# Five edits to a planned attention, expert and gated kernel: first relus on the raw table, a bias half issued later, key low parts by heads, early ups of two kept units, another order of the last tiles

## The chip, the cores and the metric

The kernel runs on one core of a Trainium2 chip. The metric is the time of one execution on the device, in microseconds (us). The kernel before has a median of 791.35 us over three runs (790.55 to 793.41). PE is the matrix engine, PEld its weight loads, DVE the vector engine, ACT the scalar engine, POOL the GpSimd engine, SP the engine whose queue issues nearly all DMAs.

## The reference

Three layers follow each other. Attention has 2 batches, 8 heads, 576 positions and head size 64, with a learned bias on relative distance:

```python
x = (psi_rel / psi_i)[..., None]          # log1p(|i-j|) / log1p(max(i,1))
h = np.maximum(x @ w1 + b1, 0.0)          # 32 hidden units
bias = h @ w2                             # one value per head
scores = scores + bias.transpose(2, 0, 1)[None, :, :, :]
attn = softmax(scores)                    # then attn @ v
```

Its output, 1152 tokens by 512, goes through four experts, `out += p_e * (relu(x @ w1[e]) @ w2[e])` with 1024 hidden units each and normalised weights p, and then through `(x @ w_a * x @ w_b) @ w_out` with 1536 hidden units. All of it is float32.

## The kernel before

**Planner.** `Plan.run` simulates the engines with estimated durations and writes out each engine's instructions in the order it arrives at. Every step is registered by `op` with its engines and their estimates, what it reads and writes, a priority (lower goes first), a number of steps it must come after (`after`) and buffers from rooms that are given out in the order in which they were asked for. On the chip each engine runs its list strictly in order and waits on semaphores only for data. So a change of one step can alter the list of every engine, and an instruction that waits holds all that stand behind it on its engine. DMAs of the SP queue are such a list too.

**Bias.** Since x is a quotient, the hidden layer of one query row is a per-row scale times the relu of w1·log + b1·psi. The log table (`tab`, 128 partitions by 576) is multiplied once by w1. A bias unit `u` is 16 query rows; 36 units make the bias, eight of them (`bias0`) the first 128 rows. `bias_group` makes for each unit four tiles `hh` (4 rows by 32 hidden units on the partitions): on DVE as max(table, −b1·psi), one of the four on ACT as a relu in most units. Four groups of matmuls (`pb`) contract with w2, `put` scales by 1/psi (`rinv`) and adds a correction (`corr`) for the part that max leaves out, `mirror` copies the reversed half, and SP stores the unit to DRAM (`bias_d`). A `bt` tile is read back skewed from there, 128 query rows and two heads; the first one is read in two halves of 64 rows, the first from units 0 to 3, the second from units 4 to 7.

**Attention.** `plain` and `qk_plain` make the first 128 query rows (t = 0) of all 4 pairs of heads and 2 batches from plain float32 keys. The later rows (t = 1 to 4) use keys and queries split into a high and a low part (`keys`, `queries`): a cast `k` and a subtraction for the low part on partitions 64 to 127, with both heads of the pair side by side along 1152 columns. `step` does scores `ps`, DVE adds the bias and takes the minimum of the negated sum (`pr`, `sums`), ACT takes the exponential, PE transposes (`pt`), copies go to `ptb`, and `values` makes `pv`, the product `xf` with the reciprocals, and the high and low parts `x_h`, `x_l` of the layer's output.

**Experts.** A unit of expert weights is 512 KB for the way up and 512 KB for the way down, each split into high and low parts (`wh`, `wl`). `up` multiplies three products of parts, twelve matmuls for 128 hidden units and one stretch of tokens, into one of the `u` banks; `relu` takes the result on ACT (high) and DVE (low, `hl`); `down` makes `pz`, six matmuls per 128 tokens; the sums go to `acc`. Tokens 0 to 255 are the t = 0 rows. Expert work has the priority of filling: PE takes it where nothing of the attention is ready. The two kept units (expert 3, quarters 3 and 2) keep their weights from the first pass to the second; the ups of the second pass for tokens 256 to 511 need only one batch of attention, those for the last 640 tokens need all of it. `x_sums` prepares sums of token blocks on DVE for the units after that (seven products instead of eight).

**Gated layer.** `x2_pair` transposes two 128-token tiles of `acc` (`px`) and makes high and low parts of blocks and of their sums and differences on ACT and DVE; `ab_item` multiplies seven products into `pw`, `pq` and `pr`, lifts them with ACT (`ct<-pw`), combines them on DVE, and `out_item` does the last `pz`. The three pairs of the last 640 tokens (tiles 6, then 4 with 7, then 5 with 8) come first, then two of the first 512 tokens.

Of the kernel before, what the change touches and what calls it, by code (L numbers as in the profile page):

```python
# [9 lines left out]
F32 = mybir.dt.float32  # L10
# [3 lines left out]
ALU = mybir.AluOpType  # L14
# [40 lines left out]
def f(ap):  # L55
    return ap.bitcast(F32)
# [175 lines left out]
def tile_kernel(ctx, tc, qd, kd, kf, vd, cst, probs, w1r, w2r, war, wbr, wor, out):  # L232
# [106 lines left out]
    def scales(e):  # L339
        nc.vector.tensor_scalar(out=pos, in0=neg_.rearrange("p (u g) -> p u g", g=4)[:, :, 4 - pos.shape[2]:], scalar1=cw[:, 1:2], scalar2=None, op0=ALU.mult)  # L340
        nc.vector.tensor_scalar(out=neg_, in0=neg_, scalar1=cw[:, 1:2], scalar2=-1.0, op0=ALU.mult, op1=ALU.mult)
        nc.vector.tensor_scalar(out=w2s, in0=w2s, scalar1=8.0, scalar2=None, op0=ALU.mult)

    lg = Buf(t=cs_t)
    op({"ACT": S / 1.2 + 200}, lambda e: nc.scalar.activation(out=tab, in_=tab, func=AF.Copy, scale=cw[:, 0:1]), r=[cs], w=[lg], prio=-1)
    op({"DVE": 450}, scales, r=[cs], w=[lg])
    cs = lg
# [6 lines left out]

    def corr_copy(e):
        for n, x in corr.items():
            nc.vector.tensor_copy(x, pc.t[:, 0:1])
            for g in range(4 - n, 4):
                nc.vector.memset(x[32 * g:32 * g + 32], 0.0)
# [5 lines left out]
    rows, early = [], []  # L365

    def bias_group(u, rank):
# [3 lines left out]
        for g in range(4):  # L371
            G = 4 * u + g
            hh = new("hh")
            hs.append(hh)
            if g < 4 - acts:
                op({"DVE": n / 1.92 + 130}, lambda e, hh=hh, G=G: nc.vector.tensor_scalar(out=hh.t[:, :n], in0=tab[:, :n], scalar1=neg_[:, G:G + 1], scalar2=None, op0=ALU.max), r=[cs], w=[hh], prio=pri, lock=True)  # L376
            else:
                op({"ACT": n / 1.2 + 220}, lambda e, hh=hh, G=G: nc.scalar.activation(out=hh.t[:, :n], in_=tab[:, :n], func=AF.Relu, bias=pos[:, u, g - 4:][:, :1]), r=[cs], w=[hh], prio=pri)
# [37 lines left out]
        side = op({e: v + 95 for e, v in t_psum(n, ENGINES["side"]).items()}, lambda e: put(e, *ends()[0]), r=[pb, cr], w=[bst], prio=pri)  # L416
# [7 lines left out]
        if u == P // 16 - 1:  # L424
            early.append(o)

# [39 lines left out]
    def bias_tile(m, t):  # L466
# [449 lines left out]
    def w2_item(p, e, c, q, h, prio=RANK["fill"]):  # L916
# [9 lines left out]
        for tt in range(nt):  # L926
# [209 lines left out]
    op({"DVE": 400}, corr_copy, r=[pc], w=[cr])  # L1136
# [50 lines left out]
    for i in (2, 0, 1):  # L1187
        x2_pair(1, i)
# [176 lines left out]
```

## Time and profile before

| | |
|---|---|
| median of 3 runs | 791.35 us (790.55 to 793.41) |
| the profiled execution | 791.38 us, span of its instructions 789.6 us |
| PE busy, matmuls | 774.2 us, 98%, 4933 instructions |
| PEld busy | 662.3 us, 84% |
| DVE / ACT / POOL busy | 649.5 us (82%) / 404.3 us (51%) / 28.1 us (4%) |
| granted PE clock | full speed in every slice |
| chain that ended last | PE 90%, DVE 6%, ACT, DMA and issue 1% each |

Matmuls are pipelined and their ends are modelled, so a busy PE includes some time in which the next matmul was late. The span has four stretches: bias and first attention rows (to about 63 us), the other attention rows among expert work (to 281 us), experts (to about 574 us), the gated layer.

### The profile page before, as it was taken

What the parts mean: (1) busy time and instruction counts of PE and PEld (TensorE: products, weight loads), DVE (VectorE), ACT (ScalarE), POOL (GpSimd) and SP (SyncE); (2) the same over time, 40 slices, a digit from 0 to 9 for tenths busy, and PEclk for the clock granted to TensorE, in tenths of its full rate; (3) what the DMA queues carried; (4) which work ended last, traced back from release to release, by engine and by line L of the source; (5) the groups of instructions that cost most, each with busy time, mean ns of one, the idle gap of its engine ahead of it and who ended that gap; (6) DMA issues with size and microseconds to landing.
All of it is one profiled execution on the core that took longest, in us unless ns stands there. A gap on an engine that the chain in (4) does not pass through costs nothing.

```text
span 789.6 us, 13146 instructions
## 1 busy us (share of the span) xinstructions
PE 774.2 (98%) x4933; PEld 662.3 (84%) x4933; DVE 649.5 (82%) x1374; ACT 404.3 (51%) x848; POOL 28.1 (4%) x46
## 2 busy tenths in 40 slices
PE   7998999999999999999999999999999999999997
PEld 3475678888988888888888888889889999999996
DVE  7899986889896687998989998988698985757545
ACT  6877765677766543544544535344466532433321
POOL 0000100000000000000000000010010100000000
PEclk9999999999999999999999999999999999999999
DMA  6996658677563134455545653545405340301103
GB/s 233 327 344 215 232 178 276 218 243 244 179 208 98 45 96 127 134 166 175 160 126 159 204 175 120 166 132 161 134 1 183 112 160 1 107 27 55 54 1 120
DMA packets 46432, 120.31 MB, mean 152 GB/s; under 512 B 5024, under 2 KB 9376, under 8 KB 46368
## 3 DMA queue, kind: packets, MB, share of 16 engines
q1 hardware_dynamic: 46224, 119.34, 46.6%
q8 instruction: 39, 0.64, 0.3%
q14 instruction: 25, 0.20, 0.1%
q10 hardware_dynamic: 144, 0.13, 0.0%
HBM read 93.62 MB, written 25.84 MB: 151 GB/s over the span
## 4 chain that ended last, share of the span: by engine, by line
PE 90%; DVE 6%; ACT 1%; issue 1%; DMA 1%; DVEq 0%; ACTq 0%
PE pz L785 32%; PE up L883 14%; PE pw L1030 9%; PE up L772 8%; PE pb L390 4%; PE pv L613 4%; PE pr L1030 4%; PE ps L513 4%; PE pt L548 4%; PE pq L1030 2%; PE ps L531 1%; PE pz L1110 1%; DVE pr L516 1%; DVE k L453 1%; PE rp L593 1%
## 5 line engine op out<-in xcount | busy, mean ns | idle before, releaser
L785 PE MATMUL pz<-wh,hh 128*128 128x512 f32 x386 | 153.2, 397 | 0.0
L785 PE MATMUL pz<-wh,hl 128*128 128x512 f32 x386 | 151.3, 392 | 0.0
L785 PE MATMUL pz<-wl,hh 128*128 128x512 f32 x386 | 151.2, 392 | 0.0
L785 PEld LDWEIGHTS pz<-wl,hh 128*128 128x128 f32 x386 | 72.5, 188 | 15.9
L785 PEld LDWEIGHTS pz<-wh,hh 128*128 128x128 f32 x386 | 72.5, 188 | 14.2 <-issue 1.8
L785 PEld LDWEIGHTS pz<-wh,hl 128*128 128x128 f32 x386 | 72.5, 188 | 12.2
L239 ACT COPY ct<-pw 128x640 f32<-128x640 f32 (+3 forms) x48 | 27.9, 582 | 85.0 <-PE pw L1030 85.0
L516 DVE CUSTOM_DVE_ANT_0 pr<-ps,bt 128x576 f32<-128x576 f32 (+1 forms) x80 | 59.9, 753 | 13.9 <-PE ps L513 11.3
L658 DVE TENSOR_TENSOR wl<-wst,wh 128x1024 fp32r<-128x1024 f32 (+1 forms) x60 | 69.7, 1162 | 1.9 <-ACT wh L239 1.6
L526 ACT ACTIVATE pr<-pr,sums 128x576 f32<-128x576 f32 x72 | 56.1, 780 | 15.3 <-DVE sums L516 10.4
L772 PE MATMUL up<-x_h,wh 128*128 128x256 f32 (+1 forms) x200 | 61.7, 308 | 0.7 <-DVE hl L796 0.7
L239 ACT CAST wh<-wst 128x1024 fp32r<-128x1024 f32 (+1 forms) x56 | 54.5, 974 | 15.1 <-PE pz L785 7.8
L772 PE MATMUL up<-x_h,wl 128*128 128x256 f32 (+1 forms) x200 | 57.3, 286 | 0.0
L772 PE MATMUL up<-x_l,wh 128*128 128x256 f32 (+1 forms) x200 | 57.2, 286 | 0.0
L239 ACT COPY ptb<-pt 128x512 f32<-128x512 f32 (+3 forms) x98 | 40.3, 438 | 30.8 <-PE pt L548 25.4
L376 DVE TENSOR_SCALAR hh<-cs 128x560 f32<-128x560 f32 (+17 forms) x112 | 43.9, 448 | 3.8 <-PE pb L390 3.6
L239 ACT COPY ct<-up 128x448 f32<-128x448 f32 x39 | 20.7, 531 | 47.8 <-PE up L883 47.6
L613 PE MATMUL pv<-ptb,v 128*64 128x128 f32 (+2 forms) x480 | 44.1, 331 | 0.3 <-ACT bst L408 0.3
L883 PE MATMUL up<-xb,wsh 128*128 128x448 f32 x156 | 44.3, 365 | 0.0
L1125 DVE TENSOR_TENSOR acc<-pz,acc 128x512 f32<-128x512 f32 x44 | 30.2, 689 | 15.9 <-PE pz L785 14.9
L772 PEld LDWEIGHTS up<-x_h,wh 128*128 128x128 f32 x200 | 37.6, 188 | 6.5 <-issue 3.0
L548 PE MATMUL pt<-ident,pr 128*128 128x128 f32 x288 | 41.7, 275 | 0.0
(194 smaller groups left out, 1844.8 us busy)
## 6 DMA issues: line engine op xcount, KB each, us to landing
wst<-in_w1r SPq DMA_DIRECT2D x30, 512.0 KB, 4.4
wst<-in_w2r SPq DMA_DIRECT2D x30, 512.0 KB, 4.5
bias_d<-bst SPq DMA_DIRECT2D x36, 295.5 KB, 4.1
bt<-bias_d SPq DMA_DIRECT2D x15, 576.0 KB, 5.3
v<-in_vd SPq DMA_DIRECT2D x24, 320.0 KB, 4.3
s<-in_war SPq DMA_DIRECT2D x12, 512.0 KB, 4.9
wz_d<-hl SPq DMA_DIRECT2D x24, 256.0 KB, 2.5
s<-in_wbr SPq DMA_DIRECT2D x12, 512.0 KB, 4.9
```

The source lines that it names most:

```text
L239: (nc.scalar.copy if e == "ACT" else engine[e].tensor_copy)(out, in_)
L376: op({"DVE": n / 1.92 + 130}, lambda e, hh=hh, G=G: nc.vector.tensor_scalar(out=hh.t[:, :n], in0=tab[:, :n], scalar1=neg_[:, G:G + 1], sca ...
L390: nc.tensor.matmul(t[32 * g:32 * g + 32, o + lo:o + hi], w2s, hs[g].t[:, lo:hi], start=True, stop=True)
L516: nc.vector.tensor_tensor_reduce(out=pr.t[r0:r1, c].rearrange("p (a b) -> p a b", a=2), in0=ps.t[r0:r1, :, :HS], in1=bt.t[r0:r1, c].rearra ...
L526: nc.scalar.activation(out=pr.t[:, c], in_=pr.t[:, c], func=AF.Exp, scale=-1.0, bias=sums.t[:, neg:neg + 1], accum_out=sums.t[:, col:col + 1])
L548: nc.tensor.transpose(pt.t[:, kt * P:kt * P + P], pr.t[:, s, k0:k0 + P], ident)
L613: nc.tensor.matmul(pv.t[s * D:(s + 1) * D, :w], V.t[:, s, kt * D:(kt + 1) * D], ptb.t[:, blk, :w], start=(kt == 0), stop=(kt == 4))
L658: op(t_two(1024 - skip, ENGINES["wlo"]), lambda e: engine[e].tensor_tensor(out=w.t[1][:, skip:], in0=wst.t[:, skip:], in1=f(w.t[0][:, skip ...
L772: nc.tensor.matmul(u.t[:, :n], block(a, ft, d), x_at(x, d, lo, n), start=(d == 0 and j == 0), stop=(d == 3 and j == 2))
L785: nc.tensor.matmul(z.t, a[:, ft, tt * P:(tt + 1) * P], bb[:, ft, :], start=(first and ft == 0 and j == 0), stop=(final and ft == 1 and j = ...
L883: nc.tensor.matmul(bank.t[:, :n], s(a, k), x(b, k), start=(first and k == 0 and i == 0), stop=(stop and k == 1 and i == 2), skip_group_che ...
L1030: nc.tensor.matmul(o_, s[:, k], d[:, k], start=(first and k == 0 and i == 0), stop=(k == 1 and i == 2), skip_group_check=True)
```

## The change

Names: `raw` is the log table as it is loaded, `tab` now a tile of its own.

1. The first bias unit takes the raw table: DVE multiplies by w1 and takes the maximum in one instruction, ACT multiplies inside its relu. The scaled table is made on ACT after that relu, for units 1 to 35. −b1·psi goes to a tile of its own, b1·psi (`pos`) moves from DVE to ACT. The factor 8 moves from w2 to `rinv` and `corr`; the zeros of `corr` are set on POOL at the start.
2. The read of the first `bt` half is registered as coming after the store of unit 6.
3. The subtraction for the low part of the keys is two steps, one for each head, 576 columns each.
4. For the first kept unit the ups of tokens 256 to 511 of both kept units are registered before the ups of the last 640 tokens.
5. The downs of the last unit of the second pass take the last five tiles in the order 4, 7, 6, 5, 8 instead of 4 to 8, and the pairs of `x2_pair` follow as (4, 7), 6, (5, 8).

```diff
+    psi, neg_ = neg_, hp.tile([P, NG], F32, name="neg")
+    op({"DVE": 290}, lambda e: nc.vector.tensor_scalar(out=neg_, in0=psi, scalar1=cw[:, 1:2], scalar2=-1.0, op0=ALU.mult, op1=ALU.mult), r=[cs], w=[NEG], prio=-1)
+    op({"ACT": 250}, lambda e: nc.scalar.activation(out=pos, in_=psi.rearrange("p (u g) -> p u g", g=4)[:, :, 4 - pos.shape[2]:], func=AF.Copy, scale=cw[:, 1:2]), r=[cs], w=[POS], prio=-1)
+    op({"DVE": 90}, lambda e: nc.vector.tensor_scalar(out=rinv, in0=rinv, scalar1=8.0, scalar2=None, op0=ALU.mult), r=[cs], w=[RI], prio=0.1)
+    raw, tab = tab, hp.tile([P, S], F32, name="tab")
+    def table():
+        op({"ACT": S / 1.2 + 200}, lambda e: nc.scalar.activation(out=tab, in_=raw, func=AF.Copy, scale=cw[:, 0:1]), r=[cs], w=[lg], prio=-0.5, after=first)
...
     def corr_copy(e):
         for n, x in corr.items():
-            nc.vector.tensor_copy(x, pc.t[:, 0:1])
-            for g in range(4 - n, 4):
-                nc.vector.memset(x[32 * g:32 * g + 32], 0.0)
+            nc.vector.tensor_scalar(out=x[:P - 32 * n], in0=pc.t[:P - 32 * n, 0:1], scalar1=8.0, scalar2=None, op0=ALU.mult)
...
+            if u == 0 and g < 4 - acts:
+                op({"DVE": n / 1.92 + 190}, lambda e, hh=hh, G=G: nc.vector.tensor_scalar(out=hh.t[:, :n], in0=raw[:, :n], scalar1=cw[:, 0:1], scalar2=neg_[:, G:G + 1], op0=ALU.mult, op1=ALU.max), r=[cs, NEG], w=[hh], prio=pri, lock=True)
+            elif u == 0:
+                first.append(op({"ACT": n / 1.2 + 220}, lambda e, hh=hh, G=G: nc.scalar.activation(out=hh.t[:, :n], in_=raw[:, :n], func=AF.Relu, scale=cw[:, 0:1], bias=pos[:, u, g - 4:][:, :1]), r=[cs, POS], w=[hh], prio=pri))
+                table()
...
+        if u == P // 16 - 2:
+            sixth.append(o)
...
-        op(t_two(2 * S, ENGINES["ksub"]), lambda e: engine[e].tensor_tensor(out=k.t[D:P], in0=k2.t[D:P], in1=f(k.t[D:P]), op=ALU.subtract), r=[k2], rw=[k], prio=RANK["prep"], lock=True)
+        whole = list(k.writers)
+        for s in range(2):
+            op(t_two(S, ENGINES["ksub"]), lambda e, s=s: engine[e].tensor_tensor(out=k.t[D:P, s], in0=k2.t[D:P, s], in1=f(k.t[D:P, s]), op=ALU.subtract), r=[k2], w=[k], after=whole, prio=RANK["prep"], lock=True)
...
-                op({"SP": 440}, lambda e, h=h, r=r: nc.sync.dma_start(out=bt.t[r], in_=bias_rows(D * h, D, 0, 2)), r=rows[4 * h:4 * h + 4], w=[bt], size=D * 8 * S)
+                op({"SP": 440}, lambda e, h=h, r=r: nc.sync.dma_start(out=bt.t[r], in_=bias_rows(D * h, D, 0, 2)), r=rows[4 * h:4 * h + 4], w=[bt], size=D * 8 * S, after=sixth)
...
-        for tt in range(nt):
+        for tt in (0, 3, 2, 1, 4) if p and c == 2 and last and e == es[-1] else range(nt):
...
-                weights(1, e, q)
-                h1[q] = w1_item(1, e, 1, q)
+                for x in KEPT if (e, q) == KEPT[0] else [(e, q)][(e, q) in KEPT:]:
+                    weights(1, *x)
+                    h1[x[1]] = w1_item(1, e, 1, x[1])
...
-    for i in (2, 0, 1):
+    for i in (0, 2, 1):
         x2_pair(1, i)
```

DVE at its start, from the first instruction after the tables have landed (`pos` and `cs` are written from the constants' tile; `hh` are the bias tiles of units 0 and 1). Before:

```order
L340 TENSOR_SCALAR pos<-cs 128x36
L341 TENSOR_SCALAR cs<-cs 128x144
L342 TENSOR_SCALAR cs<-cs 128x32
L376 TENSOR_SCALAR hh<-cs 128x576 x3
L376 TENSOR_SCALAR hh<-cs 128x560 x4
L357 COPY corr_101<-pc 128x1
L357 COPY corr_102<-pc 128x1
L359 MEMSET corr_102 32x1
```

The same stretch of DVE in the changed kernel:

```order
L341 TENSOR_SCALAR neg<-cs 128x144
L343 TENSOR_SCALAR cs<-cs 128x36
L380 TENSOR_SCALAR hh<-cs,neg 128x576 x3
L363 TENSOR_SCALAR corr_101<-pc 128x1
L363 TENSOR_SCALAR corr_102<-pc 96x1
L385 TENSOR_SCALAR hh<-tab,neg 128x560 x4
```

Three small instructions became two, the first three `hh` read the raw table, and the correction stands before unit 1 instead of behind it.

The SP queue from the first values to the full bias tiles (`bias_d<-bst` are the stores of the units in order, the 64-row `bt` the two halves). Before:

```order
L633 DMA v<-in_vd 128x640 x2
L421 DMA bias_d<-bst 128x591 x6
L487 DMA bt<-bias_d 64x2x576
L421 DMA bias_d<-bst 128x591 x4
L487 DMA bt<-bias_d 64x2x576
L476 DMA bt<-bias_d 128x2x576 x2
```

The same stretch of SP in the changed kernel:

```order
L646 DMA v<-in_vd 128x640 x2
L430 DMA bias_d<-bst 128x591 x9
L500 DMA bt<-bias_d 64x2x576
L430 DMA bias_d<-bst 128x591
L500 DMA bt<-bias_d 64x2x576
L489 DMA bt<-bias_d 128x2x576 x2
```

The first half moved from behind the store of unit 5 to behind that of unit 8; the second half stays behind the store of unit 9.

DVE at the end of the t = 0 rows (`xf`, `x_h`, `x_l` belong to the last heads of t = 0, `k` to the split keys; ISA `pr` is the first sum of scores and bias with t = 1). Before:

```order
L461 TENSOR_TENSOR ql<-q_747,qh 128x512
L376 TENSOR_SCALAR hh<-cs 128x320
L239 CAST k<-k_756 128x1152
L376 TENSOR_SCALAR hh<-cs 128x320
L453 TENSOR_TENSOR k<-k_756,k 64x1152
L618 TENSOR_TENSOR xf<-pv,rb 128x128
L376 TENSOR_SCALAR hh<-cs 128x320
L239 CAST x_h<-xf 128x128
L376 TENSOR_SCALAR hh<-cs 128x336
L621 TENSOR_TENSOR x_l<-xf,x_h 128x128
L516 ISA pr,sums<-ps,bt 128x576
```

The same stretch of DVE in the changed kernel:

```order
L634 TENSOR_TENSOR x_l<-xf,x_h 128x128
L385 TENSOR_SCALAR hh<-tab,neg 128x304
L239 CAST k<-k_763 128x1152
L385 TENSOR_SCALAR hh<-tab,neg 128x304
L466 TENSOR_TENSOR k<-k_763,k 64x576 x2
L385 TENSOR_SCALAR hh<-tab,neg 128x320 x2
L466 TENSOR_TENSOR k<-k_772,k 64x576
L809 SCALAR_TENSOR_TENSOR hl<-up,hh 128x256
L466 TENSOR_TENSOR k<-k_772,k 64x576
L529 ISA pr,sums<-ps,bt 128x576
```

The last `x_l` of t = 0 stood five instructions behind the keys' low part and now stands ahead of the keys' cast; an `hl` of expert work stands among the low parts of the second keys.

On PE the changed list has 24 up matmuls between the last `pv` of t = 0 and the first `ps` with t = 1, where the list before has none; 36 stand before the second `ps`, where before it had 6. At the end of the attention 42 fill matmuls stand between the last `pv` and the first up of the last 640 tokens, where before there were none. In the gated layer the last `px` of the 640 tokens is followed by 24 `pz` matmuls before the first `pw`, where before it was 42. The put of unit 7 moves from DVE to ACT and its mirror from ACT to DVE.

## Rows read from the trace of the kernel before

**Rows 1.** Page, part 1: busy time and share of PE, PEld.

```profile
PE 774.2 (98%) x4933; PEld 662.3 (84%) x4933; DVE 649.5 (82%) x1374; ACT 404.3 (51%) x848; POOL 28.1 (4%) x46
```

**Rows 2.** Windows: stretch, length, busy PE PEld DVE ACT POOL, clock, DMA share.

```profile
30.00:60.00 30.00, 29.75 (x304) 20.95 (x302) 28.93 (x99) 24.66 (x64) 0.85 (x2) 1.00 0.99 352
60.00:70.00 10.00, 7.69 (x74) 6.19 (x70) 9.74 (x26) 8.53 (x18) 0.41 (x1) 1.00 0.59 218
70.00:130.00 60.00, 60.00 (x467) 42.39 (x468) 49.87 (x107) 41.91 (x79) 6.03 (x11) 1.00 0.65 219
300.00:580.00 280.00, 280.00 (x1350) 244.23 (x1349) 248.40 (x483) 127.07 (x247) 2.34 (x2) 1.00 0.49 150
```

**Rows 3.** Waits of PE, whole span: sum, times, longest.

```profile
PE pc L353 <- DVE cs L342: 4.8, 1, 4.8
...
PE ps L513 <- DVE k L453: 1.1, 1, 1.1
```

**Rows 4.** Timeline of DVE and ACT from 4 us: start, duration.

```profile
4.02 0.25 DVE L340 TENSOR_SCALAR pos<-cs 128x36 f32<-128x36 f32 x1 [4.02 <-DMA cs<-in_cst]
4.31 0.29 DVE L341 TENSOR_SCALAR cs<-cs 128x144 f32<-128x144 f32 x1
...
4.83 3.06 DVE L376 TENSOR_SCALAR hh<-cs 128x576 f32<-128x576 f32 x7
...
4.02 0.78 ACT L345 ACTIVATE cs<-cs 128x576 f32<-128x576 f32 x1 [1.79 <-DMA cs<-in_cst]
```

**Rows 5.** Groups by form: two DVE operations with constants; one with a per-partition scalar.

```profile
L688 DVE TENSOR_SCALAR t<-t 128x512 f32<-128x512 f32 x36 | 16.1, 451 | 0.8 <-ACT t L702 0.7
L376 DVE TENSOR_SCALAR hh<-cs 128x512 f32<-128x512 f32 x6 | 2.6, 480 | 0.2 <-PE pb L390 0.2
```

**Rows 6.** Timeline of SP and DVE: first half, store of unit 7, second half, first scores.

```profile
18.51 0.71 SPq L487 DMA_DIRECT2D bt<-bias_d  x1
...
19.90 0.42 SPq L421 DMA_DIRECT2D bias_d<-bst  x1
...
24.21 0.61 SPq L487 DMA_DIRECT2D bt<-bias_d  x1
...
28.15 0.76 DVE L516 CUSTOM_DVE_ANT_0 pr<-ps,bt 128x576 f32<-128x576 f32 x1 [1.96 <-DMA bt<-bias_d]
```

**Rows 7.** DMA issues, KB, us to landing: store of unit 0, then of unit 7.

```profile
bias_d<-bst SPq DMA_DIRECT2D x1, 295.5 KB, 2.1
...
bias_d<-bst SPq DMA_DIRECT2D x1, 295.5 KB, 4.2
```

**Rows 8.** Timeline of PE and DVE at the end of t = 0.

```profile
62.91 0.53 PE L513 MATMUL ps<-k,qh 128*128 128x288 f32 x2 [1.14 <-DVE k L453]
...
64.97 0.53 PE L513 MATMUL ps<-k,qh 128*128 128x288 f32 x2 [0.58 <-DVE sums L516]
...
61.50 1.35 DVE L453 TENSOR_TENSOR k<-k,k 64x1152 fp32r<-64x1152 f32 x1
...
63.83 0.29 DVE L621 TENSOR_TENSOR x_l<-xf,x_h 128x128 fp32r<-128x128 f32 x1
```

**Rows 9.** Chain in order of time: 24 ups of 256 tokens; 24 downs.

```profile
132.76 2.83 PE up L772 x24
...
613.59 5.48 PE pz L785 x24
```

**Rows 10.** Timeline of PE: an up after the attention's end.

```profile
286.94 0.42 PE L772 MATMUL up<-x_h,wh 128*128 128x320 f32 x1 [0.46 <-DVE hl L796]
```

**Rows 11.** Timeline of PE and DVE: last pair of the 640 tokens, first products, lift.

```profile
563.50 0.82 PE L970 MATMUL px<-ident,acc 128*128 128x128 f32 x6
...
571.88 0.68 DVE L996 TENSOR_TENSOR x_l<-px,x_h 128x512 fp32r<-128x512 f32 x1
...
573.74 0.30 PE L1030 MATMUL pw<-x_h,wh 128*128 128x320 f32 x1
...
585.49 0.42 PE L1030 MATMUL pw<-x_h,wh 128*128 128x320 f32 x1 [1.06 <-ACT ct L239]
```

More of the change, by code (lines that the diff above doesn't have):

```diff
@@ L337, in tile_kernel @@
     op({"SP": 440}, lambda e: nc.sync.dma_start(out=cs_t, in_=cst), w=[cs], size=P * 3160)
[L339 to L347, printed above, removed]
+    psi, neg_ = neg_, hp.tile([P, NG], F32, name="neg")
+    NEG, POS, RI = Buf(t=neg_), Buf(t=pos), Buf(t=cs_t)
+    op({"DVE": 290}, lambda e: nc.vector.tensor_scalar(out=neg_, in0=psi, scalar1=cw[:, 1:2], scalar2=-1.0, op0=ALU.mult, op1=ALU.mult), r=[cs], w=[NEG], prio=-1)
+    op({"ACT": 250}, lambda e: nc.scalar.activation(out=pos, in_=psi.rearrange("p (u g) -> p u g", g=4)[:, :, 4 - pos.shape[2]:], func=AF.Copy, scale=cw[:, 1:2]), r=[cs], w=[POS], prio=-1)
+    op({"DVE": 90}, lambda e: nc.vector.tensor_scalar(out=rinv, in0=rinv, scalar1=8.0, scalar2=None, op0=ALU.mult), r=[cs], w=[RI], prio=0.1)
+    raw, tab = tab, hp.tile([P, S], F32, name="tab")
+    lg = Buf(t=tab)
+    def table():
+        op({"ACT": S / 1.2 + 200}, lambda e: nc.scalar.activation(out=tab, in_=raw, func=AF.Copy, scale=cw[:, 0:1]), r=[cs], w=[lg], prio=-0.5, after=first)
+    first = []
     pc, cr = new("tv", "pc"), Buf(t=cs_t)
@@ L353, in corr_mm @@
             nc.tensor.matmul(pc.t[32 * g:32 * g + 32, 0:1], w2s, cw[:, 1:2], start=True, stop=True)
+    for n, x in corr.items():
+        nc.gpsimd.memset(x, 0.0)
     def corr_copy(e):
         for n, x in corr.items():
-            nc.vector.tensor_copy(x, pc.t[:, 0:1])
-            for g in range(4 - n, 4):
-                nc.vector.memset(x[32 * g:32 * g + 32], 0.0)
+            nc.vector.tensor_scalar(out=x[:P - 32 * n], in0=pc.t[:P - 32 * n, 0:1], scalar1=8.0, scalar2=None, op0=ALU.mult)
     def dist(u):
@@ L363, in dist @@
         return before, after, max(before + 1, after)
-    rows, early = [], []
+    rows, early, sixth = [], [], []
     def bias_group(u, rank):
@@ L374, in bias_group @@
             hs.append(hh)
-            if g < 4 - acts:
-                op({"DVE": n / 1.92 + 130}, lambda e, hh=hh, G=G: nc.vector.tensor_scalar(out=hh.t[:, :n], in0=tab[:, :n], scalar1=neg_[:, G:G + 1], scalar2=None, op0=ALU.max), r=[cs], w=[hh], prio=pri, lock=True)
+            if u == 0 and g < 4 - acts:
[3 more added lines that the diff above has]
+                table()
+            elif g < 4 - acts:
+                op({"DVE": n / 1.92 + 130}, lambda e, hh=hh, G=G: nc.vector.tensor_scalar(out=hh.t[:, :n], in0=tab[:, :n], scalar1=neg_[:, G:G + 1], scalar2=None, op0=ALU.max), r=[lg, NEG], w=[hh], prio=pri, lock=True)
             else:
-                op({"ACT": n / 1.2 + 220}, lambda e, hh=hh, G=G: nc.scalar.activation(out=hh.t[:, :n], in_=tab[:, :n], func=AF.Relu, bias=pos[:, u, g - 4:][:, :1]), r=[cs], w=[hh], prio=pri)
+                op({"ACT": n / 1.2 + 220}, lambda e, hh=hh, G=G: nc.scalar.activation(out=hh.t[:, :n], in_=tab[:, :n], func=AF.Relu, bias=pos[:, u, g - 4:][:, :1]), r=[lg, POS], w=[hh], prio=pri)
         pb = new("tv" if n <= 512 else "s", "pb")
@@ L415, in bias_group @@
         m = min(before, after - 1)
-        side = op({e: v + 95 for e, v in t_psum(n, ENGINES["side"]).items()}, lambda e: put(e, *ends()[0]), r=[pb, cr], w=[bst], prio=pri)
+        side = op({e: v + 95 for e, v in t_psum(n, ENGINES["side"]).items()}, lambda e: put(e, *ends()[0]), r=[pb, cr, RI], w=[bst], prio=pri)
         op({e: v for e, v in {"POOL": 2 * m + 150, "ACT": m / 1.2 + 95, "DVE": m / 0.96 + 68}.items() if e in ENGINES["mirror0" if rank == "bias0" else "mirror"].split()}, mirror, w=[bst], after=[side], prio=pri)
@@ L1135, in tile_kernel @@
     op({"PE": 600}, corr_mm, r=[cs], w=[pc])
-    op({"DVE": 400}, corr_copy, r=[pc], w=[cr])
+    op({"DVE": 200}, corr_copy, r=[pc], w=[cr])
     for u in range(NU):
```

## The prediction

> **What bounds the kernel now.** I read the page's busy times first: PE is busy 98% of the span, so only 789.6 − 774.2 = 15.4 us of idle time is visible [rows 1]. Then the windows, to see where it lies. From 300 to 580 us PE is busy without a break and its weight loads take 244.23 of 280 us, 87% [rows 2]: there is nothing to win there. From 60 to 70 us PE is busy for 7.69 of 10 us while DVE is busy for 9.74, and from 30 to 60 us DVE has 28.93 of 30 us and the DMA engines a share of 0.99 [rows 2]. So the first stretch belongs to DVE and the transfers, the long rest to PE. The waits of PE name the single stalls: 4.8 us until the tables are there, 1.1 us for the keys' low part [rows 3]; the timelines give the others. The clock stands at 1.00 in every stretch shown [rows 2], so no step is priced for it.
>
> A time saved before about 63 us moves everything behind it, if PE has work at once; a time saved later counts only where PE waits. PE's instructions are the same in number and shape in both kernels, so the sum is one of waits.
>
> **First relus on the raw table.** The tables land at 4.02. DVE makes three small scalings and then stands until ACT has scaled the table (0.78 us), so its first maximum starts at 4.83 [rows 4]. Now it makes two small scalings; the first of them cost 4.31 − 4.02 = 0.29 from start to start [rows 4], so the maxima start at about 4.5, 0.3 earlier. Against that each of the three has a second scalar read per partition, a form that the trace lacks on operands in on-chip memory. The nearest row is an operation with two constants, 451 ns for 512 columns, where one with a single per-partition scalar takes 480 [rows 5]: the second step of arithmetic is free there. If the second scalar halved the rate, each would double: seven take 3.06, 0.44 each [rows 4], so three would lose 1.3 us. I take 0.1 in all, by the nearest row. The scaled table is needed after these three, at about 5.9; ACT makes its small scaling, its relu and the table, 0.25 + 0.78 + 0.78 behind 4.02 by the durations of like rows [rows 4], done at 5.8. It is hidden, with 0.1 us to spare; where it isn't, DVE waits by tenths. Net 0.2 us, between −1.0 and 0.5. The zeros of the correction on POOL, the factor 8 on other tiles and the correction ahead of unit 1 replace as much as they add.
>
> **The bias half behind more stores.** The first scores start on DVE at 28.15, after 1.96 us of waiting for the second half of the bias tile [rows 6]. That half is issued at 24.21, because it needs the store of unit 7 to have landed: issued at 19.90, it took 4.2 us, to 24.1 [rows 6, 7]. The first half's read stood right ahead, issued at 18.51 and holding SP for 0.71 [rows 6]. The store of unit 0, ahead of any read of the bias, landed in 2.1 us [rows 7]. In the new list the read goes behind the store of unit 8, so unit 7's has only stores ahead. It can't go much earlier, though: its put is now on ACT behind a relu, and its mirror waits on DVE. I put it at 19.7, and its landing between the two rows, at 3.3 us: 23.0. So the second half goes 1.2 us earlier and the scores 1.1 us earlier, the 0.2 of the table included in the 19.7. At most it is 28.15 − 1.96 = 26.2, when DVE is out of work: 2.0 us. At least nothing, if the first half, now issued at about 21.6, delays the second as it delayed the stores before. What follows from 30 to 60 us runs on transfers (share 0.99, [rows 2]) that all stand behind these halves on SP, so it moves with them. **Term 1: 1.1 us (0 to 2.0).**
>
> The Trainium skill, DMA: Bandwidth & Descriptors, section "Anatomy of one DMA", says that some 2 us of a DMA are fixed, mostly the receipt for the write, and heaviest where HBM is the target. The 2.1 us of unit 0 agrees, the 4.2 of unit 7 doesn't [rows 7]. By the rule as the whole cost the second half would go at about 22, and the term would be 2.0; I keep 1.1, from the rows.
>
> **Key low parts by heads.** PE waits 1.14 us at 62.91 for the low part, one instruction of 1.35 us for both heads, and 0.58 us at 64.97 for DVE [rows 8]. The split alone would let the first head go 0.67 earlier at the price of one more small start on DVE. But the larger change is in the order. Before, the last `x_l` of t = 0 is written at 63.83, behind the low part [rows 8], so no up could be finished earlier; now it stands ahead of the cast, and PE has 24 ups between the last `pv` and the first scores with t = 1. 24 ups take 2.83 us [rows 9]; PE was idle for 10 − 7.69 = 2.31 us in this stretch [rows 2]. The ups aren't free of waits: there are two banks for them, and the third set of twelve waits for an `hl` that stands on DVE behind three low parts of 0.67 each; with it the second scores wait, queued behind these twelve. So I count not 2.83 but most of the idle time, 2.0 us. At most 36 ups, 4.2 us by the same row, are gained; at least nothing, if DVE (83% busy from 70 to 130 us by 49.87 of 60, [rows 2]) sets the pace of what follows and PE stands later for what it gained now. **Term 2: 2.0 us (0 to 4.2).**
>
> **Both kept units' ups first.** Before, the ups of the last 640 tokens follow the last `pv` directly, while DVE makes sums of tokens; one up waits 0.46 us for an `hl` [rows 10]. With 42 matmuls in between, the conversions have time. **Term 3: 0.5 us (0 to 0.9).**
>
> **Order of the last tiles.** Before, the `px` of the last pair start by 563.50; its first low part starts at 571.88, ends at 572.56, and the first product goes at 573.74, behind 42 downs [rows 11]: 8.6 us from the end of the `px` (564.0), of which the pair spends most in line behind the other two. Now there are only 24 downs, 5.48 us [rows 9], for it. If the 8.6 stayed, PE would stall 3.1 us. But the pair of two tiles comes first now and is converted while 18 downs run, so the last one should find ACT and DVE free: I take no stall. Later, at 585.49, PE waits 1.06 us for a lift on ACT behind casts [rows 11]. In the new lists the difference that those casts need comes earlier; a lift itself can't be hidden there, so I take 0.4 of it. **Term 4: 0.4 us (−3.1 to 1.1).**
>
> **Sum.** 1.1 + 2.0 + 0.5 + 0.4 = 4.0. The profiled execution took 791.38 us (span 789.6), the median of the runs is 791.35: the sum goes against 791.4 and gives 787.4 us. What a measurement here can tell from no change is about 0.5%, 4.0 us: the forecast lies on that bound.
>
> **Rivals.** *The gain at 60 us is given back.* DVE and ACT feed the attention until about 130 us, and PE's lead over them shrinks as buffers fill. For it: DVE's 9.74 of 10 us [rows 2]. Against it: 83% afterwards, and expert work that needs little of DVE. Term 2 is then about 0.2, and the time 791.4 − 2.2 = 789.2.
>
> *PE has more slack than its busy time shows.* From 70 to 130 us PE counts as busy for all 60 us, but its weight loads for only 42.39, 71% against 87% later [rows 2]; that would be up to 9 us in which matmuls came late, though the bias's matmuls load only 32 columns of weights and explain part. A new order with an early lead of PE may close some: term 2 reaches 4.2, and the time is 791.4 − 6.2 = 785.2. The Trainium skill, Perfetto Trace Analysis, section "Identifying the Most-Contended Engine", says that busy matmuls are a poor measure of PE's headroom and the share of weight loads a good one. These two rows bear it out.
>
> *The attention falls behind and the fill runs out (the other side).* The ups now stand ahead of scores in PE's list. If each of the 16 later groups lost the wait computed above for the third twelve, about 0.9 us (three low parts of 0.67 less a first block of scores and the products between), the attention would end 14 us late; 42 matmuls, some 6 us, are left as fill. PE would idle 8 us before the last ups: 791.4 − 1.1 − 0.4 + 8 = 797.9. It makes the kernel slower from a lateness of about 8 us on. For it: one up waits there already [rows 10]. Against it: fewer matmuls stand ahead of the last `pv` than before.
>
> *The edits do little.* The first half delays the second where it now stands, and the last pair stalls PE by up to 3.1: 791.4 − 2.0 − 0.5 + 3.1 = 792.0 at worst, about 791 in the middle.
>
> **How the numbers follow.** The forecast has 0.45, half of it either side of its bound (own range 785.8 to 789.0): 0.24 faster, 0.21 same. Given back: 0.18, same. More slack: 0.17, faster. Little: 0.08, same. Attention late: 0.12, of which 0.11 slower and 0.01 same. So faster by over 0.5% 0.41, within 0.5% 0.48, slower 0.11. The range runs from 784.6, a little under the second rival, to 791.6, over the first and most of the last; what lies outside is the late attention and the tails, under 0.2.
>
> **What would show it.** Right: first scores on DVE at about 27.0; the second half issued near 23; PE from 60 to 70 us busy for 9 us or more, without a wait over 0.3 for the keys; no wait at the first ups of the last 640 tokens; first `pw` directly behind the downs. Wrong: a doubled duration of the three maxima on the raw table; the second half issued at 24 or landing after 28; PE waiting for `hl` between 60 and 130 us by more than 2 us in all; a wait of `pw` for `x_l` near 570 us; the last `pv` later than 281 us.

## The result: slower by 4.9 us, where 4.0 us less was predicted

The changed kernel takes 796.86 us (median of 6 runs, 795.60 to 799.43), the kernel before 791.97 us beside it (6 runs, 790.55 to 793.41). The ratio is 1.0061, with a 95% interval from 1.0045 to 1.0076. The forecast was 787.4 us and its range ended at 791.6. A median mixes executions with and without a short fall of PE's clock (last section): of 94 of the kernel before, the 35 with a mean clock of 0.998 or less have a median of 792.8 us, the others 791.2.

The page of the changed kernel (columns as in [rows 1]), from an execution of 798.19 us with a span of 796.4:

```profile
PE 779.2 (98%) x4933; PEld 663.0 (83%) x4933; DVE 651.5 (82%) x1398; ACT 401.3 (50%) x834; POOL 32.2 (4%) x45
```

PE has the same 4933 matmuls and seems as busy as before, 98%. That row hides the loss, since a matmul that comes late counts as busy. The windows show more (columns as in [rows 2]):

```profile
28.00:30.00 2.00, 0.70 (x4) 0.34 (x5) 1.56 (x5) 0.76 (x2) 0.00 (x0) 1.00 1.05 393
30.00:31.00 1.00, 1.00 (x8) 0.61 (x7) 1.00 (x3) 1.00 (x5) 0.00 (x0) 0.93 1.05 391
31.00:32.00 1.00, 1.00 (x7) 1.00 (x6) 0.97 (x6) 1.00 (x3) 0.00 (x0) 0.50 1.09 412
32.00:34.00 2.00, 2.00 (x9) 1.37 (x9) 0.94 (x4) 1.44 (x4) 0.00 (x0) 0.50 1.00 356
...
60.00:70.00 10.00, 9.17 (x86) 7.23 (x83) 9.67 (x27) 7.41 (x16) 0.00 (x0) 1.00 0.74 283
70.00:130.00 60.00, 59.27 (x459) 39.90 (x457) 52.01 (x114) 46.37 (x90) 8.78 (x10) 1.00 0.71 231
130.00:200.00 70.00, 67.75 (x511) 58.48 (x511) 59.49 (x141) 43.85 (x99) 2.67 (x4) 1.00 0.67 214
```

The last stretch in the kernel before:

```profile
130.00:200.00 70.00, 69.85 (x525) 61.80 (x524) 62.44 (x128) 47.87 (x115) 1.94 (x3) 1.00 0.76 246
```

The hole from 60 to 70 us is filled, 9.17 us busy against 7.69. But from 70 to 200 us PE does fewer matmuls (970 against 992), loads weights for 98.4 us against 104.2, and stands still for 3.0 us against 0.15. The first scores didn't come earlier either. SP, then DVE (start, duration; answers to [rows 6]; the first row holds the stores of units 7 and 8, the third the tenth store, that of unit 9):

```profile
19.56 1.56 SPq L430 DMA_DIRECT2D bias_d<-bst  x2
21.22 0.71 SPq L500 DMA_DIRECT2D bt<-bias_d  x1
23.73 0.33 SPq L430 DMA_DIRECT2D bias_d<-bst  x1
24.23 0.61 SPq L500 DMA_DIRECT2D bt<-bias_d  x1
...
28.43 0.76 DVE L529 CUSTOM_DVE_ANT_0 pr<-ps,bt 128x576 f32<-128x576 f32 x1 [1.79 <-DMA bt<-bias_d]
```

The second half goes at 24.23, as before, though the store of unit 7 had landed at 21.65. It stands on SP behind the tenth store, and that one waited for the mirror copy of its unit, which the new list has put on POOL. POOL's copy, and SP's wait for it from 15 to 25 us:

```profile
21.98 1.73 POOL L239 COPY bst<-bst 128x159 f32<-128x159 f32 x1 [20.59 <-ACT bst L417]
SPq L430 <- POOL bst L239: 1.8, 1, 1.8
```

In the kernel before ACT made this copy, and the tenth store went at 22.24:

```profile
21.89 0.33 ACT L239 COPY bst<-bst 128x159 f32<-128x159 f32 x1
```

The waits of PE over the whole span (answer to [rows 3]) are many small ones on what DVE and ACT make:

```profile
PE pc L356 <- DMA cs<-in_cst: 4.3, 1, 4.3
PE up L785 <- DVE hl L809: 2.0, 3, 0.9
PE ps L544 <- issue: 1.5, 1, 1.5
PE pw L1043 <- DVE ct L1068: 1.0, 1, 1.0
PE pw L1043 <- ACT ct L239: 0.8, 1, 0.8
PE pv L626 <- DVE ptb L239: 0.7, 2, 0.4
```

One of them shows how such a wait comes about. DVE and PE from 129 us, in the changed kernel:

```profile
129.49 0.69 DVE L239 CAST wh<-wst 128x1024 fp32r<-128x1024 f32 x1 [2.16 <-PE up L785]
130.10 1.22 DVE L671 TENSOR_TENSOR wl<-wst,wh 128x1024 fp32r<-128x1024 f32 x1
131.23 0.75 DVE L809 SCALAR_TENSOR_TENSOR hl<-up,hh 128x256 fp32r<-128x256 f32 x2
131.71 0.39 PE L785 MATMUL up<-x_h,wh 128*128 128x256 f32 x1 [0.85 <-DVE hl L809]
```

PE has filled both banks with ups. The `hl` that would free one is ready to be computed at 129.9, but the list has put a weight's cast and low part ahead of it on DVE, and PE stands for 0.85 us. DVE was not short of time here: it had itself stood for 2.16 us before that cast, until PE's ups were through. It is the order that costs here.

**A measure that counts late matmuls.** For the comparisons below I cut PE's instructions into blocks of one operation and shape. A block lasts until the next one starts. Its excess is that time less its count times the pace of the fastest fifth of such blocks in the trace before. The excess of a stretch holds waits, slow starts and a lower clock alike. In us, by stretch:

```
              0-28  28-36 36-60 60-70 70-200 200-280 280-300 300-560 560-640 640-  sum
before        15.1   1.3   3.1   3.1   15.9    7.0     1.4     3.4     3.8   2.4  56.6
after         15.9   2.4   2.7   1.3   21.9    7.8     0.4     3.9     4.5   3.0  63.8
start_only    15.9   1.1   2.3   2.1   20.6    6.4     0.4     3.8     4.6   2.7  59.9
split_only    14.2   1.4   3.5   3.2   19.3    6.9     1.3     3.8     2.8   2.8  59.1
kept_only     13.9   1.4   4.1   3.0   16.0    7.0     1.1     3.9     5.0   3.0  58.3
tiles_only    14.9   1.3   3.1   3.1   16.1    6.9     1.4     3.2     4.0   2.8  56.8
n_settle      14.9   2.6   3.4   2.5   21.2    7.5     0.5     3.3     3.0   2.9  61.9
n_corr        14.1   1.4   4.2   1.5   19.7    7.3     0.4     3.2     2.9   2.9  57.5
n_act149      14.7   1.3   3.2   4.0   17.9    7.7     0.7     3.3     3.0   2.6  58.3
raw_held      15.0   1.5   4.2   2.9   16.0    7.0     1.4     3.4     3.8   2.9  58.2
split_held    14.1   1.4   3.5   2.7   15.9    7.1     1.3     3.5     3.6   2.8  55.7
half_first    14.3   1.2   2.1   2.9   20.7    7.7     0.2     3.8     3.6   2.9  59.4
hyb_a         14.0   1.4   4.1   3.0   16.1    6.9     1.4     3.4     3.7   2.7  56.6
lite_before   14.8   1.3   3.7   1.9   15.0    6.7     1.2     3.5     3.5   2.8  54.5
lite_after    16.0   1.1   2.3   2.9   19.3    6.8     0.2     3.3     4.1   2.9  58.7
raw_only      16.2   2.2   2.7   1.6   21.0    6.3     0.6     3.3     4.9   2.8  61.7
hyb_b         14.6   1.4   3.5   2.7   16.2    7.1     1.2     3.4     3.6   2.8  56.5
hyb_c         15.7   1.3   3.1   3.0   16.1    6.9     1.4     3.2     3.7   2.8  57.2
```

The sums differ by 7.2 us between before and after, the two executions by 6.8. Of that 6.0 us lie from 70 to 200 us, in the attention with its fill, where the prediction had no term. From 60 to 70 us 1.8 us are won, from 280 to 300 us 1.0. How far one trace can be trusted, the table shows too: the eight in which PE has the list of before up to 200 us with nothing taken from its work (before, kept_only, tiles_only, raw_held, split_held and the three hyb) lie between 15.9 and 16.2 from 70 to 200 us. Two traces of another list there differ by more: 21.9 and 20.7 (after, half_first), 20.6 and 21.0 (start_only, raw_only).

### The profile page after: what moved, and what is told of

Read it like the earlier page. It is cut to its first block, busy times and chain, and to the rows that moved or that the text cites. A ratio compares the mean times of both kernels' runs of the same rounds, so it can differ in the third digit from the quotient of the medians.

```text
span 796.4 us, 13154 instructions
## 1 busy us (share of the span) xinstructions
PE 779.2 (98%) x4933; PEld 663.0 (83%) x4933; DVE 651.5 (82%) x1398; ACT 401.3 (50%) x834; POOL 32.2 (4%) x45
## 4 chain that ended last, share of the span: by engine, by line
PE 87%; DVE 7%; DMA 2%; ACT 2%; issue 2%; DVEq 0%; SPq 0%
PE pz L798 32%; PE up L896 13%; PE pw L1043 9%; PE up L785 8%; PE pv L626 4%; PE pr L1043 4%; PE pb L399 4%; PE pt L561 4%; PE ps L526 4%; PE pq L1043 2%; PE ps L544 1%; DMA wst<-wz_d 1%; DVE pr L529 1%; PE pz L1123 1%; DVE wl L671 1%
## 5 line engine op out<-in xcount | busy, mean ns | idle before, releaser
L798 PEld LDWEIGHTS pz<-wl,hh 128*128 128x128 f32 x386 | 72.4, 188 | 15.9
L239 ACT CAST wh<-wst 128x1024 fp32r<-128x1024 f32 (+1 forms) x54 | 52.3, 968 | 13.1 <-PE pz L798 8.8
L808 ACT ACTIVATE hh<-up 128x256 fp32r<-128x256 f32 (+2 forms) x76 | 27.8, 381 | 41.2 <-PE up L785 30.2
L385 DVE TENSOR_SCALAR hh<-tab,neg 128x544 f32<-128x544 f32 (+17 forms) x109 | 42.0, 443 | 4.4 <-PE pb L399 4.3
L239 ACT COPY ct<-up 128x448 f32<-128x448 f32 x39 | 20.7, 531 | 49.3 <-PE up L896 49.2
## 6 DMA issues: line engine op xcount, KB each, us to landing
bias_d<-bst SPq DMA_DIRECT2D x36, 295.5 KB, 3.6
```

The lines of the kernel that those rows point to most:

```text
L239: (nc.scalar.copy if e == "ACT" else engine[e].tensor_copy)(out, in_)
L798: nc.tensor.matmul(z.t, a[:, ft, tt * P:(tt + 1) * P], bb[:, ft, :], start=(first and ft == 0 and j == 0), stop=(final and ft == 1 and j = ...
```

## The experiments

All times are medians; a ratio is against the kernel before in the same session (791.39 to 791.96 us).

**Each part alone.** The change's diff was put on the kernel before piece by piece: the raw table with the bias half behind the seventh store (start_only), the raw table without that (raw_only), the key's low part by heads (split_only), both kept units' ups first (kept_only), the order of the last tiles and pairs (tiles_only).

```diff
# raw_only differs from start_only by
-                op({"SP": 440}, ..., r=rows[4 * h:4 * h + 4], w=[bt], size=D * 8 * S, after=sixth)
+                op({"SP": 440}, ..., r=rows[4 * h:4 * h + 4], w=[bt], size=D * 8 * S)
```

> The kernel before with the raw-table relus and the bias half behind seven stores, nothing else. Theory A (the loss of 4.9 us sits in the order of the fill work between 100 and 282 us and is not made by the start): the first scores stay near 28.4 us, so 791 to 793, with a dip of the granted clock near 31 us in some executions worth 2 to 3 us. Rival B (the start makes the loss, by the clock and by what it delays): 794.5 to 797.5.

> The raw-table relus alone; PE and DVE keep the list of the run with both parts of the start, only the bias half goes behind six stores and not nine. Theory A: the same as start_only within 1 us, because the second half's landing decides the first scores and stays at 28 to 28.5 us. Rival (the half behind nine stores costs or gains by itself): a difference of 1 us or more, in the sense of where the second half lands.

> The kernel before with the key low parts by heads, nothing else; the list of PE changes from its 299th instruction. Theory A: the changed order of the fill loses what the split gains, 793 to 796. Rival B: 789 to 791, the 2 us that PE was idle from 60 to 70 us.

> The kernel before with the ups of both kept units first, nothing else; PE's list changes only from its 1687th instruction. Theory A: no wait at the first ups of the last 640 tokens, but a changed order of the fill: 791 to 794. Rival B: 790.5 to 791.5, the 0.5 us alone.

> The kernel before with the order of the last tiles and of the last three pairs alone; PE's list is that of before up to its 3057th instruction. Theory L (lists cost; here little is dealt anew): the stretch 560 to 640 us moves by -0.4 to +1.3 us, the rest not, 791.0 to 792.7. Rival P (the new order of the pairs by itself brings the wait behind the weights' sums near 624 us): 792.4 or more.

Measured: start_only 794.47 (1.0042, 1.0027 to 1.0057); raw_only 795.17 (1.0047, 1.0030 to 1.0063); split_only 793.78 (1.0034, 1.0023 to 1.0046); kept_only 793.35 (1.0019, 1.0009 to 1.0028); tiles_only 790.95 (0.9987, 0.9977 to 0.9997). All but the last are slower, by 1.8 to 3.6 us, and they don't add up: start, split and kept together would be 6.9. Theory A put the loss on the order of the fill and left the start at 791 to 793; the start alone costs 2.9, so that form of it fell. The number is nearly rival B's (from 794.5), but not its reason: the loss is not at the start. To 28 us there is 0.8 more excess, from 70 to 200 us 4.7 more, and the clock stood at 1.0 in all four runs. split_only loses 3.4 in that stretch. kept_only leaves it alone, as its list differs only later, and loses 1.2 from 560 to 640 us. So the same stretch loses from edits that have nothing in common but that the planner then hands out another list. (raw_only lies within 1 us of start_only and split_only and kept_only in their ranges, all as theory A had it; tiles_only is just below theory L's range.) That called for lists without any edit.

**New lists, no edit.** One number of the planner is changed. PE's instructions stay the same, but by a comparison of the lists some 700 to 760 of them stand elsewhere, about as many as with the start alone (some 720) or the split alone (some 650). What the planner hands out includes the engine for some of the small steps: DVE has 1380 instructions in n_settle, 1375 in n_corr and 1393 in n_act149, where before it has 1374, and ACT and POOL have that many fewer in sum. So "not one instruction is altered", below, holds for the steps and not for where each runs.

```diff
-    SETTLE = {"PE": 210, "ACT": 150, "DVE": 140, "POOL": 120}
+    SETTLE = {"PE": 210, "ACT": 150, "DVE": 141, "POOL": 120}   # n_settle
+    SETTLE = {"PE": 210, "ACT": 149, "DVE": 140, "POOL": 120}   # n_act149
-    op({"DVE": 400}, corr_copy, r=[pc], w=[cr])
+    op({"DVE": 200}, corr_copy, r=[pc], w=[cr])                 # n_corr
```

> The kernel before with one number of the planner raised by 1 ns (what it adds behind each instruction of DVE); not one instruction is added, removed or altered, but the planner hands out another list, in which some 700 of PE's instructions stand elsewhere, as many as with the start alone or the split alone. Theory L (the list is what costs: the one of before is a lucky one, and any edit deals a new one): 792.5 to 795.5, with the excess at 70 to 200 us or 560 to 640 us. Rival P (each part costs by its own instructions): within 0.7 us of before.

> The kernel before with one planning number changed, 400 to 200 ns for the correction's copies, which the change also brings; no instruction is altered and some 700 of PE's stand elsewhere. Theory L: a second new list, slower again, 792.3 to 796. Rival (the list of the 1 ns was an unlucky draw and lists do not differ on average): 790 to 792.

> A third list without an altered instruction: the planner's number behind each instruction of ACT is 149 ns instead of 150; some 760 of PE's instructions stand elsewhere. Theory L: slower than before, by 0.8 to 4.5 us, with the excess from 70 to 200 us at 18.5 us or more against 15.9. Rival: not slower by more than 0.7 us.

Measured: n_settle 795.43 (1.0057, 1.0042 to 1.0072), n_corr 793.07 (1.0013, 1.0003 to 1.0023), n_act149 794.01 (1.0023, 1.0014 to 1.0033). A planning number of 141 instead of 140 ns costs 4.0 us, nearly as much as the whole change. All three are slower, and all three in the stretch from 70 to 200 us, by 5.3, 3.8 and 2.0; the last is less than I expected (18.5 or more, 17.9 came). n_settle, windows:

```profile
70.00:130.00 60.00, 59.77 (x463) 41.12 (x460) 52.42 (x115) 43.51 (x87) 7.50 (x9) 1.00 0.66 215
130.00:200.00 70.00, 67.02 (x497) 58.94 (x497) 59.54 (x129) 42.61 (x96) 2.68 (x4) 1.00 0.71 234
```

It looks like the changed kernel: 3.2 us of standing in 130 us, but by another wait. Waits of PE there, n_settle:

```profile
PE ps L513 <- DVE sums L516: 2.3, 3, 1.3
PE up L772 <- DVE hl L796: 0.5, 2, 0.2
```

**The parts in the list of before.** The same instructions, but given out within the old operations with the old costs, so that PE's list stays as it was, word for word.

```diff
# split_held: one operation of the planner, two instructions
-  lambda e: engine[e].tensor_tensor(out=k.t[D:P], ...)
+  lambda e: [engine[e].tensor_tensor(out=k.t[D:P, s], ...) for s in range(2)]
# raw_held: unit 0 reads the raw table; the table is made behind its relu on ACT
-  nc.vector.tensor_scalar(out=hh.t[:, :n], in0=tab[:, :n], scalar1=neg_[...], op0=ALU.max)
+  nc.vector.tensor_scalar(out=hh.t[:, :n], in0=raw[:, :n], scalar1=cw[:, 0:1], scalar2=neg_[...], op0=ALU.mult, op1=ALU.max) if u == 0 else ...
```

> The key low part as two instructions of one head each, in the list of before word for word (PE's list is unchanged). Theory L: the split by itself is worth 0 to 0.7 us either way, 790.8 to 792.3, against 793.8 with the list that it deals. Rival P: the eight more starts on DVE cost, 793 to 794.

> The raw-table part in the list of before (PE's list is unchanged; DVE loses its scaling of 36 columns and some small settings). Theory L: the start is earlier by 0.2 to 0.4 us and the time 790.8 to 791.8. Rival P: 793.5 to 795, as in the runs with the start alone.

Measured: raw_held 791.45 (1.0003, 0.9994 to 1.0013), split_held 792.56 (1.0017, 1.0006 to 1.0028). The raw table costs 3.6 us with the list that it deals and nothing that shows in the old one: that settles it for this part. The split is not settled: 792.56 lies in neither range. Five of its 10 runs took 790.75 to 792.04 and five 793.08 to 794.04, four of these at a lower mean clock (0.998); its trace, of the fastest, has the least excess of all but the lightened one. In it the first scores with t = 1 wait 0.54 us where [rows 8] have 1.14, but the next ones wait for DVE's sums 1.13 where they had 0.58:

```profile
60.94 0.53 PE L513 MATMUL ps<-k,qh 128*128 128x288 f32 x2 [0.54 <-DVE k L453]
...
63.55 0.53 PE L513 MATMUL ps<-k,qh 128*128 128x288 f32 x2 [1.13 <-DVE sums L516]
```

**The half ahead of the tenth store.** Only SP's order is changed, in the changed kernel.

```diff
         def store(e):
+            if u == 9 and not held:
+                held.append(store)        # given out by the second half
+                return
...
+                    if h:
+                        held[0](e)        # the tenth store, behind the second half
```

> The changed kernel with one exchange on SP: the read of the second bias half ahead of the tenth store instead of behind it; all other engines keep their lists. In the changed kernel the half waited on SP from 21.65, when the eighth store had landed, until the tenth store was issued at 23.73. Theory Q (that queue place is why the start did not get earlier): the half is issued at 22.0, lands at 25.7 to 26.2, the first scores start near 26.2 instead of 28.4, and the time falls by 1 to 2.2 us to 793.5 to 795. Rival (the transfers at 30 to 60 us set the pace anyway): within 0.7 us of the changed kernel, 795 to 797.

Measured: 794.07 (1.0039, 1.0024 to 1.0053; the changed kernel has 1.0061, 1.0045 to 1.0076). Its SP (both halves, then the tenth store), then DVE:

```profile
20.87 1.48 SPq L504 DMA_DIRECT2D bt<-bias_d  x2
23.38 0.34 SPq L433 DMA_DIRECT2D bias_d<-bst  x1
...
26.22 0.76 DVE L537 CUSTOM_DVE_ANT_0 pr<-ps,bt 128x576 f32<-128x576 f32 x1
```

The first scores start at 26.22 and wait for nothing; with the half behind the tenth store they start at 28.43, 28.24 and 28.08 in three traces (after, start_only, lite_after). The time falls by some 2 us, as theory Q had it, though the two intervals still overlap. So the queue place, with the late store in it, had kept the gain away; that such a gain lasts, the next runs show more firmly.

**What gains, put together in the list of before.** hyb_a is raw_held with both halves behind the ninth store and ahead of the tenth; hyb_b has the split in it too, hyb_c the order of the last tiles.

```diff
             nc.sync.dma_start(out=bias_d[16 * u:16 * u + 16, ...], in_=bst.t[:, :before + after])
+            if u == 8:
+                held[0](e)                # the first half, kept back until here
...
+                    if h:
+                        held.append(0)
+                        held[1](e)        # the tenth store, behind the second half
```

> The list of before on PE, ACT and POOL, with the raw-table part and with both bias halves behind the ninth store and ahead of the tenth on SP. Theory Q+L (the start's gain is real once the half doesn't stand behind the tenth store and the list stays): second half issued near 21.7, first scores near 26.2, time 789.0 to 790.7, faster than before by 0.7 to 2.2 us. Rival T (from 30 to 60 us the transfers set the pace): 791 to 792.

> As hyb_a, with the key low part split as well, still in the list of before. Theory Q+L: the split takes the first scores with t = 1 some 0.5 us earlier, 788.6 to 790.5. Rival: the split's second start on DVE costs as much as it brings, equal to hyb_a within 0.5 us or slower by up to 1.2.

> As hyb_a, with the change's order of the last tiles and pairs; PE's list is that of before up to its 3057th instruction. If the gains add: 2.2 of hyb_a and 1.0 of tiles_only, 788.2 to 789.3. Rival (the gain of tiles_only was chance): within 0.4 us of hyb_a, 789.4 to 790.4.

Measured: hyb_a 789.79 (0.9971, 0.9960 to 0.9983), hyb_b 790.45 (0.9984, 0.9975 to 0.9993), hyb_c 790.00 (0.9981, 0.9969 to 0.9993). hyb_a beats both kernels, that of before by 2.2 us and the changed one by some 7. As it differs from raw_held (1.0003) in SP's order alone, the 2 us and more belong to that order. SP in it:

```profile
21.09 1.48 SPq L505 DMA_DIRECT2D bt<-bias_d  x2
22.62 0.58 SPq L432 DMA_DIRECT2D bias_d<-bst  x1
```

The first scores start at 26.45 in hyb_a, 26.56 in hyb_b and, late again, at 27.80 in hyb_c (last section). Neither the split nor the last tiles add to it: hyb_b lies in the ranges of both its theories, hyb_c in that of the rival. The gain of tiles_only doesn't come back, and whether it was one stays open.

**What a new list costs by.** DVE gets less to do, in both lists.

```diff
-  engine[e].tensor_tensor(out=w.t[1][:, skip:], in0=wst.t[:, skip:], in1=f(w.t[0][:, skip:]), op=ALU.subtract)
+  engine[e].tensor_copy(w.t[1][:, skip:], f(w.t[0][:, skip:]))
```

> The kernel before in its own list; the low part of each weight is written as a plain copy of the high part (0.68 us) instead of the difference (1.21 us), so the experts' results leave out the low part, and DVE has some 0.5 us less to do in each of the 31 between 70 and 280 us. Theory D (PE waits for DVE): the excess of PE from 70 to 200 us falls from 15.9 us, to 12 to 15, time 788 to 791. Rival S (PE's own sequence, DVE has enough air): excess within 0.7 us of 15.9, time 790.5 to 792.

> The changed kernel in its own list, with the same copy in place of the difference. Theory D: the excess of PE from 70 to 200 us falls from 21.9 us to within 2 us of lite_before, the time by 3 to 6 us, 790 to 793. Rival S: excess of 20 to 22 us, time within 1.5 us of the changed kernel, 794 to 797.

Measured: 788.90 (0.9960, 0.9946 to 0.9975) and 793.52 (1.0023, 1.0013 to 1.0034). The excess from 70 to 200 us falls by 0.9 in the old list and by 2.6 in the new one, so the two still differ by 4.3 of 6.0. Theory D asked for 2 or less, rival S for no change. That PE waits for DVE costs both kernels, then, and it explains little of the difference between them. The 1.7 us by which it shrank are not firm, since half_first, with the lists of the changed kernel but for SP's, has 20.7 without any lightening. By the medians both gain about as much, 3.0 and 3.3 us: they stay 4.6 us apart, where it was 4.9. The wait for `hl` falls from 1.7 to 0.2 us between 66 and 290 us, those for `ptb`, `bst` and sums don't. By what the rest of the list's cost comes is open: steps in line on ACT, small steps that changed engine, or PE's own sequence; none was tried.

## Why the prediction was wrong, step by step

**The missing term.** The step that failed is "PE's instructions are the same in number and shape in both kernels, so the sum is one of waits". The sum let the change move its own instructions and took the rest of the 800 us as fixed. Hundreds of PE's instructions stand elsewhere in the new list; I priced the places that the section on the change names and put the new list as a list at nothing. It cost 6.0 us from 70 to 200 us, and 4.8 in half_first, which has the same list on PE. The rival of the attention that falls behind came nearest, but by another mechanism and end: the last block of `pv` starts at 279.03, before at 279.23, and no fill ran out. Six other orders of that stretch were measured (after, start_only, split_only and the three without an edit); none is as good there as that of before, 17.9 to 21.9 against 15.9 to 16.2. Had all four terms below come in, 4.0 us, the list's price would still have outweighed them.

**Term 1, 1.1 us: not there.** The raw relus cost little more than assumed. Three take 1.56 us from 4.64, 0.33 behind the tables' landing, where before it was 0.81; that is 0.52 each against the 0.44 of [rows 4], 0.2 in all where the prediction took 0.1, and far from the doubling:

```profile
4.64 1.56 DVE L380 TENSOR_SCALAR hh<-cs,neg 128x576 f32<-128x576 f32 x3
```

The store of unit 7 landed earlier than the 23.0 of the prediction: issued at 19.56, at 21.65. That is 2.1 us, for a DMA issued on SP. The Trainium skill (DMA: Bandwidth & Descriptors, "Anatomy of one DMA") gives some 2 us as the fixed part of a DMA issued from GpSimd and adds the bytes at 436 GB/s, for 295.5 KB an estimated 0.7 us; the trace agrees with the fixed part, and these 2.1 us leave no room for the second. But the 4.2 of [rows 7] was no exception. Of the ten stores before, the first three took 2.1 us and the others 2.7 to 4.2, three of them (2.7 to 4.0) ahead of any read of the bias. So the two rows were not a pair with and without a read ahead, as the prediction took them; the store of unit 6, too, stood between the read and unit 7's.

The step that failed in this term is the one from the landing to the half's issue, "3.3 us: 23.0". SP takes its list in order, the tenth store stands ahead of the half, and it is issued only at 23.73, after the 1.73 us of the copy on POOL. That the half stays behind that store was said ahead of the prediction; the working then looked only at what the half depends on, and not at what that store waits for. The term also started from 28.15, which is the latest of five traces with the same list up to there (last section), so neither its size nor its upper end was known to a microsecond.

**Term 2, 2.0 us: right where it was looked for.** The excess from 60 to 70 us fell by 1.8. The order did it, as the prediction had it in the main, and not the split: from 36 to 70 us the excess is 6.2 before, 4.0 after, 4.4 and 4.3 in start_only and raw_only, which lack the split, and 6.7 in split_only. The loss from 70 us on is not this gain given back: split_only and n_act149 (7.2) don't have the gain and lose there as well.

**Term 3, 0.5 us: right in size, wrong in cause.** The wait at 286.94 is gone (excess 1.4 to 0.4). But in n_settle, n_corr and start_only, without this edit, the excess falls as far (0.4 or 0.5), and in kept_only, with this edit alone, a wait of 0.6 us for `hl` stays.

**Term 4, 0.4 us: near in size, wrong in cause.** No `pw` waits for `x_l`, and the wait for ACT's lift falls from 1.06 to 0.78. But it is 0.8 in split_only, without this edit, and 1.5 in tiles_only, with this edit alone. A new wait of 1.04 us stands at 628.28, for DVE:

```profile
628.28 0.41 PE L1043 MATMUL pw<-x_h,wh 128*128 128x320 f32 x1 [1.04 <-DVE ct L1068]
```

It is absent in half_first, which has the same lists but for SP's, so it comes from this execution and not from the order of the tiles; the excess there (560 to 640 us) is 3.6 in half_first, 4.5 in after.

## What to carry to other kernels

Where a planner deals out the order, measure first what a new list costs by itself: change one planning number by a nanosecond, and take the spread (here +1.1, +2.1 and +4.0 us) as the error of every prediction that moves the list. Test an edit inside the old list before judging it. In an in-order queue read everything that stands ahead of the transfer that is wanted early, and what each of these waits for, not only what the transfer itself depends on.

## What the runs showed of the hardware

**The clock after a hole.** PE's granted clock, 1.00 in the mean over the trace before, falls to 0.50, 1.2 instead of 2.4 GHz, for some 3 us where PE has stood still. In the changed kernel PE was busy for 0.70 us of 28 to 30, and the clock is at 0.50 from 31 (windows above). In kept_only, which has the list of before at that place, it is the hole from 60 to 64 us that is followed by it:

```profile
60.00:62.00 2.00, 0.86 (x13) 0.62 (x10) 1.94 (x5) 1.97 (x4) 0.00 (x0) 1.00 1.01 405
62.00:64.00 2.00, 1.46 (x11) 1.26 (x11) 1.95 (x8) 1.36 (x3) 0.00 (x0) 0.97 0.96 343
64.00:66.00 2.00, 2.00 (x12) 0.94 (x12) 1.97 (x4) 0.66 (x2) 0.00 (x0) 0.50 0.11 40
```

Not every execution has it. The changed kernel took 795.60 and 795.61 us at a mean clock of 1.000, 796.32 and 797.39 at 0.999, 798.19 and 799.43 at 0.997. The prediction wrote that no step is priced for the clock since it stood at 1.00: one trace didn't show that. half_first, without the hole at 28 us, showed 1.0 in all its four runs; but so did start_only, in whose trace PE was busy for 0.89 us of 28 to 30.

**The same list, another start.** Up to the first scores tiles_only, kept_only, split_only and split_held have the list of before. These scores started at 27.69, 27.00, 26.83 and 26.77 us in their traces, and at 28.15 in that of before. The fourth store, for one, took 2.6 us to land in kept_only and 3.95 before, which holds the first half and all behind it on SP. A wait of 1 us read from one trace of this start is thus known to no better than 1 us.

**A copy on POOL of 0.4 or 1.7 us.** POOL's first mirror copy, of 143 or 159 columns, took 0.40 to 0.52 us in eleven of the 18 traces, 1.72 or 1.73 in all five with the changed start (after, start_only, raw_only, half_first, lite_after), and 2.46 and 2.52 in n_act149 and hyb_c. Spans on POOL are rough, but each time the store that needs the copy was issued within 0.04 us of its end: at 23.73 in the changed kernel, at 22.11 in hyb_c, where it was the ninth and held back both halves. Why the same kind of copy takes so much longer there, no run shows.
